# Block sums of the output weights by adding DMAs, a ring of seven weight blocks, and loads and stores issued by GpSimd, in a one-core attention and feed-forward kernel

## The chip, the cores and the metric

The kernel runs on one core of a Trainium2 chip. The metric is the device time of one execution in microseconds, the median of several runs. The core's engines are TensorE (PE, with its weight loads as PEld), VectorE (DVE), ScalarE (ACT), GpSimd (POOL) and SyncE (SP). Each works through its own list of instructions in order, and they wait for one another by semaphores. SP does no arithmetic here: it issues DMA transfers, which sixteen DMA engines carry out.

## The reference

```python
def _attn_ref(q, k, v, n_sink, window):          # q, k, v: (4, 8, 768, 64), n_sink 4, window 128
    scores = (1.0 / np.sqrt(D)) * np.matmul(q, k.transpose(0, 1, 3, 2))
    keep = is_sink | in_window                   # key < n_sink, or 0 <= query - key < window
    a = softmax(np.where(keep, scores, -1e9))    # with 1e-9 added to the sum
    return np.matmul(a, v)

def _moe_ref(x, w_in, w_out):                    # x: (3072, 512), w_in (512, 2048), w_out (2048, 512)
    h = x @ w_in
    return (h - np.tanh(h)) @ w_out
```

The weights come in as 64-bit words that the chip decodes to 32-bit floats. All products are made at nearly full float precision: an operand is split into a rounded high part and a low rest, and three of the four partial products are added.

## The kernel before

**Tiling.** The 3072 tokens are 12 chunks of 256 (`cc`), the hidden width is 8 groups of 256 (`g`). A step is one chunk with one group, and there are 96 steps in the order of the list `order`: chunks 0 to 2 interleaved in steps 0 to 23 while the weights are still being decoded, then chunks 3 to 11 one after the other with eight steps each. A step's first half is 24 matmuls into `h` (`mm1`, line 772). Then come tanh on ACT (791), the difference on DVE (794), the rounded high part on ACT (797 or 810) and the low part on DVE (800 or 813), and the second half multiplies by the group's block of `w_out`: 12 matmuls of 512 columns (`mm2`, 842) for chunks 0 to 4, 21 matmuls of 256 columns (`mm7`, 876) for chunks 5 to 11.

**Seven products.** `mm7` uses Strassen's scheme: seven block products in place of eight. It needs sums of the four quarter blocks of each group's `w_out` (`derive`). Five new blocks a group are made: three go into `edge` tiles, which take the place of decoded `w_in` groups that are no longer needed, and two replace quarters of `w` itself. Each sum is made on DVE or GpSimd with three adds over high and low parts (980, 982, 984) in half of the tile `wide`, rounded by ACT (996), and its low rest is made by DVE (1001, 1003).

**Weights.** `weights(k, g)` decodes `w_in` (k = 0) or `w_out` (k = 1) of a group: three DVE passes (156, 158, 160) into `wm`, one of two scratch halves of the tile `pt`, then the high part on ACT (712) and the low part on DVE (716). The decoded `w_in` is stored to DRAM (`wscr`, 720), and from step 24 on it is streamed back in four blocks of 256 KB a step into a ring of five block places (`stream`, 757): four in a tile `ring`, one in `spare`. A block feeds six `h` matmuls, and its place is free when these are done.

**Attention.** Each chunk has four units (pairs of heads). A unit loads keys and queries (`load_qk`, 333 and 342), from unit 12 on splits them (`split`: ACT 468 and 478, DVE 473 for keys, GpSimd 481 for the queries' low part), makes scores (509), softmax (524 to 560), the sink columns on GpSimd (569 to 571), transposes (594) and masks (608 on DVE, 614 on GpSimd); a chunk's values follow (657), and `x` for the chunk's steps.

**Order.** All of it is put down as work items with an engine, an estimated time and a due time (`work.add`). The class `Work` walks through them once, when the program is built, takes at each moment the item with the earliest due time on each engine, and so fixes one order for every engine. Times such as `STREAM`, `DEAR`, `LEAD` and `PACE` are due times; they move instructions in that order and have no other effect. SP issues every transfer, in this one order: weights, keys, queries, values, ring blocks, and stores of results. A transfer that waits for its place holds back all those behind it.

Of the kernel before, what the change touches and what calls it, by code (L numbers as in the profile page):

```python
# [32 lines left out]
NG = 8  # L33
# [135 lines left out]
class Work:  # L169
# [7 lines left out]
    def __init__(self, slack, pad, late):  # L177
        self.all, self.wrote, self.read = [], {}, {}
        self.slack, self.pad, self.late = slack, pad, late
# [14 lines left out]
    def order(self):  # L194
# [15 lines left out]
        while any(waiting.values()):  # L210
# [6 lines left out]
            if lands:  # L217
                free[e], done[n] = t + lands, t + lands + 1700
# [14 lines left out]
def _banded(tc, qd, kp, vp, vs, masks, w_in, w_out, ident, pts, early, out):  # L233
    nc = tc.nc
    et = mybir.EngineType
    with ExitStack() as ctx:
# [5 lines left out]
        qpool, kpool, vpool, hpool = pool("qpool", 2), pool("kpool", 2), pool("vpool", 3), pool("hpool", 1)  # L242
# [14 lines left out]
        spare = gpool.tile([P, WG // 2], F32R, tag="spare", name="spare")  # L257
        wscr = dpool.tile([NG, P, 2 * WG], F32, tag="wscr", name="wscr")
        kscr = dpool.tile([2, P, 2, DM // 2], F32, tag="kscr", name="kscr")
# [4 lines left out]
        work = Work(SLK, PAD, LATE)  # L264
# [8 lines left out]
        FIRST, EARLY, PACE, LEAD = 45000.0, 4600.0, 7956.0, 43418.0  # L273
        UNIT, SECOND, WLEAD, WNEXT = 2000.0, 3000.0, 6000.0, 2500.0
        HALF2, LAST = 9148.0, 6188.0
        SPILL, STREAM, DEAR, DLATE = 47526.0, 10850.0, 120000.0, 17426.0
# [20 lines left out]
        def raw(u):  # L297
            return u < RAW
# [16 lines left out]
        def slots(u):  # L315
            i = u if u < 2 or u in lent else u % 2 + 2
            return [("kt", i), ("qt", i)]

        def load_qk(u):
            cc, p, b, c = unit(u)  # L320

            def lend():
                if lent[u] not in place_of:
# [4 lines left out]
            def keys():  # L328
                if u in lent:
# [3 lines left out]
                nc.sync.dma_start(kt[u], kp[b, p, :, 2 * c * TS : 2 * c * TS + KW])  # L333

            def queries():
# [5 lines left out]
                else:  # L341
                    nc.sync.dma_start(qt[u], src.rearrange("h d s -> d h s"))

            def zeros():
                if u in lent:
# [8 lines left out]
            work.add("SP", 500, t, keys, (), [slots(u)[0], "seq k"], lands=800)  # L354
            work.add("SP", 1000, t, queries, (), [slots(u)[1], "seq q"], lands=600 if raw(u) else 1000)
# [3 lines left out]
        def load_v(cc):  # L359
# [19 lines left out]
            work.add("SP", 500 * took, due_unit(4 * cc), values, (), [vslot[cc, i] for i in new] + ["seq v"],  # L379
# [312 lines left out]
        def weights(k, g):  # L692
# [28 lines left out]

            d = due_group(g) + WNEXT * k - WLEAD
# [630 lines left out]
```

## Time and profile before

| | us |
|---|---|
| median of 3 runs (lowest, highest) | 696.69 (695.9, 698.17) |
| profiled execution | 696.93 |
| its span, first to last instruction | 695.2 |
| PE busy in it | 663.2 |
| DVE busy | 565.3 |
| ACT busy | 411.5 |
| GpSimd busy | 175.9 |

The profiled execution's own time is its span and 1.7 us around it. PE's share says that matmuls stand nearly back to back; where PE is not busy, the list of waits names the engine or transfer that let it go on ("issue" means that the trace names none). The tables by stretch show where along the span that is.

### The profile page before, as it was taken

To read this page: it belongs to the slowest core of one execution; us is meant where nothing else is said; L and a number is where in the kernel's file an instruction comes from. 1 tells how busy PE (TensorE), PEld (TensorE's weight loads), DVE (VectorE), ACT (ScalarE), POOL (GpSimd) and SP (SyncE) were. 2 spreads that over 40 slices of the span, in tenths; PEclk is the share of its full clock that TensorE was granted. 3 is DMA by queue.
4 is the path that set the end of the run, shared out by engine and by line. 5 is a ranking of instruction groups with operands and counts; after the bars stand their busy time and mean duration, and the time that the engine had idled before them with its cause. 6 is when DMAs were issued, how large, how long until landed. Compare 5 with 4: busy or idle time off the path is not lost.

```text
span 695.2 us, 14415 instructions
## 1 busy us (share of the span) xinstructions
PE 663.2 (95%) x5099; PEld 609.7 (88%) x5099; DVE 565.3 (81%) x1385; ACT 411.5 (59%) x1056; POOL 175.9 (25%) x287
## 2 busy tenths in 40 slices
PE   6899999999998997999999999999999999999996
PEld 4677899999987886889999999999999998999895
DVE  6999998946888999899988878978777986985554
ACT  5985333347885665766668567567566665662221
POOL 5433000002445563313223223221112132220000
PEclk9999999999999999999999999999999999999999
DMA  5779864241257575657757857856865865654762
GB/s 180 263 258 385 314 263 154 93 148 58 79 145 229 163 212 152 197 179 219 248 178 214 279 165 205 269 180 188 264 199 169 261 212 172 188 177 132 240 192 71
DMA packets 77485, 137.23 MB, mean 197 GB/s; under 512 B 8156, under 2 KB 28764, under 8 KB 77404
## 3 DMA queue, kind: packets, MB, share of 16 engines
q1 hardware_dynamic: 77404, 136.22, 62.8%
q8 instruction: 42, 0.69, 0.4%
q14 instruction: 39, 0.32, 0.1%
HBM read 120.98 MB, written 15.20 MB: 196 GB/s over the span
## 4 chain that ended last, share of the span: by engine, by line
PE 71%; DVE 14%; ACT 6%; DMA 5%; issue 2%; POOL 1%; SPq 0%; DVEq 0%; POOLq 0%; ACTq 0%
PE h L772 29%; PE s L876 10%; PE o L876 7%; PE o L842 6%; PE s L842 3%; PE x L657 3%; DMA ring<-wscr 3%; PE t L594 2%; PE t L657 2%; PE t L842 2%; PE x L842 2%; PE t L509 1%; PE x L509 1%; DVE wide L982 1%; PE s L509 1%
## 5 line engine op out<-in xcount | busy, mean ns | idle before, releaser
L772 PE MATMUL h<-xh,ring 128*128 128x256 f32 x924 | 185.4, 282 | 8.2 <-DMA ring<-wscr 5.0
L772 PEld LDWEIGHTS h<-xh,ring 128*128 128x128 f32 x924 | 150.9, 189 | 10.4 <-DMA ring<-wscr 6.3
L772 PE MATMUL h<-xl,ring 128*128 128x256 f32 x462 | 128.8, 279 | 0.0
L791 ACT ACTIVATE gbuf<-h 128x512 f32<-128x512 f32 x96 | 57.2, 596 | 104.9 <-PE h L772 59.0
L481 POOL TENSOR_TENSOR q<-qraw,q 128x512 fp32r<-128x512 f32 x36 | 47.6, 1321 | 247.3 <-ACT q L478 247.3
L772 PEld LDWEIGHTS h<-xl,ring 128*128 128x128 f32 x462 | 87.4, 189 | 0.3
L534 ACT ACTIVATE p<-p,st 128x132 f32<-128x132 f32 x168 | 67.0, 401 | 21.5 <-DVE st L526 19.8
L810 ACT CAST ghbuf<-gbuf 128x896 fp32r<-128x896 f32 x55 | 51.8, 943 | 41.4 <-DVE gbuf L807 41.2
L813 DVE TENSOR_TENSOR glbuf<-gbuf,ghbuf 128x896 fp32r<-128x896 f32 x55 | 62.0, 1128 | 14.7 <-ACT ghbuf L810 10.7
L772 PE MATMUL h<-xh,w 128*128 128x256 f32 x384 | 73.4, 281 | 0.0
L772 PEld LDWEIGHTS h<-xh,w 128*128 128x128 f32 x384 | 60.8, 188 | 1.3 <-PE x L657 0.2
L560 ACT ACTIVATE p<-p,st 128x132 f32<-128x132 f32 x168 | 54.2, 394 | 4.1 <-DVE st L555 3.5
L794 DVE TENSOR_TENSOR gbuf<-h,gbuf 128x512 f32<-128x512 f32 x55 | 37.9, 689 | 19.4 <-ACT gbuf L791 18.9
L772 PE MATMUL h<-xl,w 128*128 128x256 f32 x192 | 53.5, 279 | 0.0
L842 PE MATMUL o<-w,ghbuf 128*128 128x512 f32 x192 | 51.5, 399 | 1.3 <-ACT ghbuf L797 1.3
L473 DVE TENSOR_TENSOR ks<-kraw,ks 64x392 fp32r<-64x392 f32 x72 | 48.2, 670 | 5.0 <-ACT ks L468 2.7
L772 PE MATMUL h<-xh,spare 128*128 128x256 f32 x228 | 50.6, 285 | 1.3 <-DMA spare<-wscr 1.3
L614 POOL TENSOR_TENSOR pt<-pt,after 128x512 f32<-128x512 f32 x32 | 43.7, 1366 | 27.7 <-ACT pt L611 25.7
L608 DVE TENSOR_TENSOR pt<-t,below 128x512 f32<-128x512 f32 (+1 forms) x48 | 28.9, 601 | 19.5 <-ACT pt L611 7.9
L569 POOL CAST z<-p 128x16 fp32r<-128x16 f32 x42 | 11.0, 261 | 119.1 <-ACT p L560 116.2
L772 PEld LDWEIGHTS h<-xh,spare 128*128 128x128 f32 x228 | 39.0, 189 | 1.8 <-DMA spare<-wscr 1.5
L842 PEld LDWEIGHTS o<-w,ghbuf 128*128 128x128 f32 x192 | 33.6, 188 | 7.2 <-ACT ghbuf L797 1.5
(173 smaller groups left out, 1659.6 us busy)
## 6 DMA issues: line engine op xcount, KB each, us to landing
ring<-wscr SPq DMA_DIRECT2D x231, 256.0 KB, 4.0
spare<-wscr SPq DMA_DIRECT2D x57, 256.0 KB, 4.0
qraw<-qd SPq DMA_DIRECT2D x36, 256.0 KB, 3.9
wraw<-w_in SPq DMA_DIRECT2D x16, 512.0 KB, 7.0
wraw<-w_out SPq DMA_DIRECT2D x16, 512.0 KB, 8.2
wscr<-w SPq DMA_DIRECT2D x16, 512.0 KB, 6.8
kraw<-kp SPq DMA_DIRECT2D x38, 196.0 KB, 3.8
v<-vp SPq DMA_DIRECT2D x27, 256.0 KB, 3.2
```

Of the source, the lines that this page charges most:

```text
L473: (nc.gpsimd if KP else nc.vector).tensor_tensor(k[o, h, :], t[r, :], k[r, h, :].bitcast(F32), op=ALU.subtract)
L481: (nc.gpsimd if QP else nc.vector).tensor_tensor(ql[u], qt[u], qh[u].bitcast(F32), op=ALU.subtract)
L534: nc.scalar.activation(e, e, AF.Exp, bias=st[u][:, j : j + 1], scale=-1.0, accum_out=st[u][:, 4 + j : 5 + j],)
L560: nc.scalar.activation(pr[u][:, j, :], pr[u][:, j, :], AF.Copy, scale=s[:, 8 + j : 9 + j])
L614: nc.gpsimd.tensor_tensor(w[:, :, 0, :], w[:, :, 0, :], after.unsqueeze(1).to_broadcast([P, 4, P]), op=ALU.mult)
L772: nc.tensor.matmul(hps[n][:, f, :], lhsT=w, rhs=x, start=r == 0, stop=r == 11)
L791: nc.scalar.activation(g0, h(), AF.Tanh)
L794: nc.vector.tensor_tensor(g0 if strassen(n) else h(), h(), g0, op=ALU.subtract)
L810: nc.scalar.copy(ghbuf[:, n % 2], gbuf[:, 1:, :])
L813: nc.vector.tensor_tensor(glbuf[:, :7, :], gbuf[:, 1:, :], ghbuf[:, n % 2].bitcast(F32), op=ALU.subtract)
L842: nc.tensor.matmul(sums_of(n, cc, t), lhsT=a[:, f, t * P : (t + 1) * P], rhs=wt[1, g][:, (0, 1, 0)[i], f, :], start=first and not low and ...
L876: nc.tensor.matmul(acc, lhsT=a[:, b, :], rhs=factor(g, m, part % 2), start=g == 0 and part == 0 and m in (4, 1, 2, 7), stop=closes(n) and ...
```

## The change

Three things change, and the due times are set anew.

1. **Block sums by transfers.** While `w_out` of a group is being decoded, three transfers store the blocks that the sums need to a new DRAM scratch `bscr`: two straight from `wm` (`spill_plus`), and one after ACT has negated half of it into `gbuf` (`negative`, `spill_minus`). The next weight that is decoded into the same half of `pt` now waits for the first two of these to land. Later `derive` makes each sum with two transfers: SP copies one block from `bscr` into the sum's own place, GpSimd issues a second transfer that adds the other block to it. ACT rounds the result, DVE makes the low rest. The adds on DVE and GpSimd and their scratch in `wide` are gone.
2. **Ring of seven.** Three block places stand in the tile `spare`, four in `ring`. To make room, keys and queries have one buffer each in place of two, and unit u + 1 is loaded where u + 2 was.
3. **Other queues.** From unit 12 on keys and queries, from chunk 4 on values, the result stores of the seven-product part (all but the last chunk's) and the reload of the kept block (`keep(True)`) are issued by GpSimd. The queries' low part goes from GpSimd to DVE (`QP` 1 to 0).

```diff
-        qpool, kpool, vpool, hpool = pool("qpool", 2), pool("kpool", 2), pool("vpool", 3), pool("hpool", 1)
+        qpool, kpool, vpool, hpool = pool("qpool", 1), pool("kpool", 1), pool("vpool", 3), pool("hpool", 1)
...
-        SLK, PAD, LATE, QP, KP, BP, LEAD3 = 0.0, 1.05, 65222.0, 1, 0, 1, 37045.0
-        SA, NSLOT, RING, GP, DP = 5, 7, 5, 0, 1
+        SLK, PAD, LATE, LAND, QP, KP, BP, LEAD3 = 0.0, 1.05, 65222.0, 4372.0, 0, 0, 1, 89032.0
+        SA, NSLOT, RING, GP, LQ, ST = 5, 7, 7, 0, 1, 1
...
-                nc.sync.dma_start(kt[u], kp[b, p, :, 2 * c * TS : 2 * c * TS + KW])
+                (nc.gpsimd if LQ and not raw(u) else nc.sync).dma_start(kt[u], kp[b, p, :, 2 * c * TS : 2 * c * TS + KW])
...
-                    nc.sync.dma_start(qt[u], src.rearrange("h d s -> d h s"))
+                    (nc.gpsimd if LQ else nc.sync).dma_start(qt[u], src.rearrange("h d s -> d h s"))
...
-                    nc.sync.dma_start(vt[cc, i], vp[b, i * P : (i + 1) * P, :])
+                    (nc.gpsimd if LQ and cc > 3 else nc.sync).dma_start(vt[cc, i], vp[b, i * P : (i + 1) * P, :])
...
+            def negative():
+                nc.scalar.activation(gbuf[:, 4:].rearrange("p b t -> p (b t)"), wm[key][:, DM:], AF.Copy, scale=-1.0)
+
+            def spill_plus():
+                nc.sync.dma_start(bscr[g][:, 0:2], wm[key][:, :DM].rearrange("p (k c) -> p k c", k=2))
+                nc.sync.dma_start(bscr[g][:, 2], wm[key][:, 3 * DM // 2 :])
+
+            def spill_minus():
+                nc.sync.dma_start(bscr[g][:, 3:5], gbuf[:, 4:].rearrange("p (k a) t -> p k (a t)", k=2))
...
+            if k:
+                work.add("ACT", 520, d + 1600, negative, [("dw", r)], ["minus"])
+                work.add("SP", 700, d + 1500, spill_plus, [("dw", r)], [("b", g, 0)], lands=1200)
+                work.add("SP", 400, d + 2200, spill_minus, ["minus"], [("b", g, 1)], lands=800)
...
-            ring[i] = spare if i == 4 else ring["a"][:, i, :]
+            if i > 3 and "b" not in ring:
+                ring["b"] = gpool.tile([P, 3, WG // 2], F32R, tag="spare", name="spare")
+            ring[i] = ring["b"][:, i - 4, :] if i > 3 else ring["a"][:, i, :]
...
+            def copied():
+                nc.sync.dma_start(block(1).bitcast(F32), bscr[g][:, x])
+
+            def added():
+                nc.gpsimd.dma_start(block(1).bitcast(F32), bscr[g][:, y], accum_op=ALU.add)
+
+            def rounded():
+                nc.scalar.activation(block(0), block(1).bitcast(F32), AF.Copy, scale=-1.0 if m == 4 else 1.0)
+
+            def rest_of():
+                lo, hi = block(1), block(0).bitcast(F32)
+                if m == 4:
+                    nc.vector.scalar_tensor_tensor(lo, lo.bitcast(F32), -1.0, hi, op0=ALU.mult, op1=ALU.subtract)
                 else:
...
+                    nc.vector.tensor_tensor(lo, lo.bitcast(F32), hi, op=ALU.subtract)
...
-                if RAW <= u + 2 < NU:
-                    load_qk(u + 2)
+                if RAW <= u + 1 < NU:
+                    load_qk(u + 1)
```

SP's order while chunk 9 is worked on (steps 78 to 82 are being loaded; `spare` and `ring` are ring blocks, `qraw`, `kraw`, `v` and `out` the loads and stores of attention and results). Before:

```order
L757 DMA ring<-wscr 128x512 x4
L342 DMA qraw_6897<-qd 128x2x256
L333 DMA kraw_6918<-kp 128x392
L757 DMA spare<-wscr 128x512
L757 DMA ring<-wscr 128x512 x3
L376 DMA v_4_7007<-vp 128x512
L376 DMA v_5_7009<-vp 128x512
L757 DMA ring<-wscr 128x512
L757 DMA spare<-wscr 128x512
L342 DMA qraw_7105<-qd 128x2x256
L757 DMA ring<-wscr 128x512 x4
```

After, at the same place:

```order
L778 DMA ring<-wscr 128x512 x4
L778 DMA spare<-wscr 128x512 x3
L778 DMA ring<-wscr 128x512 x4
L778 DMA spare<-wscr 128x512 x3
L778 DMA ring<-wscr 128x512 x4
```

Every load that stood between ring blocks has gone to GpSimd's list, and SP holds ring blocks alone there.

DVE's order around step 29, chunk 3 (`s` scores, `h` and `glbuf` the step's difference and low part, `wide` the scratch of the block sums). Before:

```order
L800 TENSOR_TENSOR glbuf<-h_2624,ghbuf 128x512
L980 TENSOR_TENSOR wide<-w_3_1227 128x512
L982 TENSOR_TENSOR wide<-wide,w_3_1227 128x512
L984 TENSOR_TENSOR wide<-wide,w_3_1227 128x512
L1003 SCALAR_TENSOR_TENSOR edge_2660<-wide,edge_2660 128x256
L1001 TENSOR_TENSOR edge_2660<-wide,edge_2660 128x256 x2
L980 TENSOR_TENSOR wide<-w_4_1333 128x512
L673 TENSOR_TENSOR xl_2786<-x,xh_2785 128x512
```

After, at the same step:

```order
L815 TENSOR_TENSOR h_2775<-h_2775,gbuf 128x512
L613 TENSOR_TENSOR pt<-t,below 128x4x128
L559 TENSOR_SCALAR st_2854<-st_2854 128x4
L560 RECIPROCAL st_2854<-st_2854 128x4
L821 TENSOR_TENSOR glbuf<-h_2775,ghbuf 128x512
L486 TENSOR_TENSOR q_2887<-qraw_2814,q_2887 128x512
L478 TENSOR_TENSOR ks_2921<-kraw_2828,ks_2921 64x392 x2
```

The adds into `wide` are gone, the low rests of the edge blocks (24 of 256 columns) now stand at steps 20 to 28, and the queries' low part (486) has joined each unit.

GpSimd's order around steps 22 and 23, where the sums' transfers are issued (`edge` with 995 is an adding transfer, `z` the sink columns, 614 and 619 the mask multiplication before and after). Before:

```order
L481 TENSOR_TENSOR q_2115<-qraw_1958,q_2115 128x512
L569 CAST z<-p_2084 128x2x8
L570 TENSOR_TENSOR z<-p_2084,z 128x2x8
L571 CAST z<-z 128x2x16
L614 TENSOR_TENSOR pt<-pt,after 128x4x128
L481 TENSOR_TENSOR q_2211<-qraw_2050,q_2211 128x512
```

After:

```order
L337 DMA kraw_2139<-kp 128x392
L995 DMA edge_2072<-bscr 128x256
L574 CAST z<-p_2052 128x2x8
L575 TENSOR_TENSOR z<-p_2052,z 128x2x8
L576 CAST z<-z 128x2x16
L619 TENSOR_TENSOR pt<-pt,after 128x4x128
L995 DMA edge_2072<-bscr 128x256 x2
L346 DMA qraw_2225<-qd 128x2x256
L995 DMA edge_2072<-bscr 128x256
L995 DMA edge_2172<-bscr 128x256
L337 DMA kraw_2263<-kp 128x392
```

Transfers that wait for a landing or for PE now stand in one line with the sink columns and masks, on which the chunk's values wait.

## Rows read from the trace of the kernel before

**Rows 1.** The page of the profile: busy time of the engines with their share of the span.

```profile
PE 663.2 (95%) x5099; PEld 609.7 (88%) x5099; DVE 565.3 (81%) x1385; ACT 411.5 (59%) x1056; POOL 175.9 (25%) x287
```

**Rows 2.** Busy time by stretch: from and to (us from the span's start), length, then busy us and instructions of PE, PEld, DVE, ACT, POOL, the granted TensorE clock, the DMA engines' busy share and GB/s.

```profile
50.00:100.00 50.00, 48.91 (x333) 42.86 (x333) 46.90 (x72) 23.76 (x47) 6.69 (x10) 1.00 0.91 343
...
150.00:200.00 50.00, 49.93 (x352) 44.34 (x351) 34.47 (x106) 37.17 (x105) 14.76 (x24) 1.00 0.26 80
...
200.00:275.00 75.00, 68.20 (x466) 59.26 (x465) 69.39 (x155) 46.87 (x130) 41.91 (x53) 0.99 0.64 191
275.00:345.00 70.00, 69.14 (x500) 63.03 (x500) 62.28 (x156) 46.35 (x122) 18.75 (x25) 0.99 0.68 206
...
475.00:660.00 185.00, 177.75 (x1530) 171.86 (x1529) 142.81 (x358) 104.10 (x249) 33.35 (x54) 1.00 0.67 202
```

**Rows 3.** PE's waits between 200 and 345 us: who was waited for, us in total, times, longest.

```profile
PE h L772 <- issue: 3.1, 1, 3.1
PE s L509 <- DVE ks L473: 1.7, 3, 0.9
PE o L842 <- ACT ghbuf L797: 1.3, 1, 1.3
PE t L509 <- DVE pt L608: 0.9, 1, 0.9
```

**Rows 4.** The timeline between 258 and 276 us (start, us, instruction; in brackets the engine's idle time before it): block-sum adds on GpSimd and DVE, the step's low part, and PE's next matmuls into `h`.

```profile
268.49 1.10 POOL L980 TENSOR_TENSOR wide<-w 128x256 f32<-128x256 f32 x1 [2.83 <-DVE edge L1001]
...
270.05 1.11 DVE L980 TENSOR_TENSOR wide<-w 128x512 f32<-128x512 f32 x1
...
272.32 0.69 DVE L984 TENSOR_TENSOR wide<-wide,w 128x512 f32<-128x512 f32 x1
272.93 0.68 DVE L800 TENSOR_TENSOR glbuf<-h,ghbuf 128x512 fp32r<-128x512 f32 x1
...
273.72 0.55 PE L772 MATMUL h<-xh,ring 128*128 128x256 f32 x1 [3.13 <-issue]
```

**Rows 5.** The stretches around that wait (columns as in rows 2), and two pieces of the chain of work that ended last: start, us, what.

```profile
270.60:273.70 3.10, 0.00 (x0) 0.01 (x1) 3.03 (x5) 0.65 (x2) 1.06 (x2) 0.93 0.52 163
273.70:276.70 3.00, 2.98 (x14) 3.00 (x15) 2.54 (x10) 2.53 (x9) 0.00 (x0) 0.50 0.05 13
...
273.72 2.90 PE h L772 x12
...
277.20 1.41 PE h L772 x12
```

**Rows 6.** DVE's groups of instructions between 200 and 345 us: the block sums' adds and the edge blocks' low rests (count, busy us, mean ns, idle before).

```profile
L982 DVE TENSOR_TENSOR wide<-wide,w 128x512 f32<-128x512 f32 x16 | 14.8, 928 | 0.4
L984 DVE TENSOR_TENSOR wide<-wide,w 128x512 f32<-128x512 f32 x16 | 14.6, 911 | 0.5
...
L980 DVE TENSOR_TENSOR wide<-w 128x512 f32<-128x512 f32 x16 | 13.2, 826 | 1.1 <-DMA out<-wide 0.9
...
L1001 DVE TENSOR_TENSOR edge<-wide,edge 128x256 fp32r<-128x256 f32 x16 | 6.1, 418 | 0.0
```

**Rows 7.** PE's waits between 345 and 660 us.

```profile
PE h L772 <- DMA ring<-wscr: 5.0, 6, 1.5
PE s L876 <- ACT ghbuf L810: 1.4, 3, 0.5
PE h L772 <- DMA spare<-wscr: 1.3, 1, 1.3
```

**Rows 8.** SP's timeline between 577 and 588 us, ahead of one of those waits (start, time to issue, transfer).

```profile
578.98 0.33 SPq L757 DMA_DIRECT2D spare<-wscr  x1
582.32 0.38 SPq L342 DMA_DIRECT2D qraw<-qd  x1
582.80 2.11 SPq L757 DMA_DIRECT2D ring<-wscr  x4
```

**Rows 9.** What SP's own queue waited for between 345 and 660 us: the loads of values (376), keys (333) and queries (342).

```profile
SPq L376 <- PE t L657: 18.7, 5, 4.3
...
SPq L333 <- DVE ks L473: 11.8, 10, 2.3
SPq L342 <- POOL q L481: 10.0, 5, 3.0
```

**Rows 10.** GpSimd's groups: the queries' low parts and the masks over the whole span.

```profile
L481 POOL TENSOR_TENSOR q<-qraw,q 128x512 fp32r<-128x512 f32 x36 | 47.6, 1321 | 247.3 <-ACT q L478 247.3
L614 POOL TENSOR_TENSOR pt<-pt,after 128x512 f32<-128x512 f32 x32 | 43.7, 1366 | 27.7 <-ACT pt L611 25.7 <-DMA spare<-wscr 0.8 <-DMA ring<-wscr 0.7
```

**Rows 11.** Landing times: stores of decoded `w_in` issued between 60 and 100 us (count, KB, median us), and all transfers from and to `wscr` over the span.

```profile
wscr<-w SPq DMA_DIRECT2D x8, 512.0 KB, 9.4
...
DMA to landing us min/median/max: 2.6/4.0/10.7
```

**Rows 12.** DVE's timeline between 66 and 100 us: the ends of a `w_out` decode (160) and the first pass of the next one (156), groups 1 to 3.

```profile
66.80 1.28 DVE L160 SCALAR_TENSOR_TENSOR pt<-wraw,pt 128x1024 uint32<-128x1024 uint32 x1
...
75.34 0.68 DVE L156 TENSOR_SCALAR pt<-wraw 128x1024 uint32<-128x1024 uint32 x1
...
78.34 1.22 DVE L160 SCALAR_TENSOR_TENSOR pt<-wraw,pt 128x1024 uint32<-128x1024 uint32 x1
...
87.14 0.68 DVE L156 TENSOR_SCALAR pt<-wraw 128x1024 uint32<-128x1024 uint32 x1
```

More of the change, by code (lines that the diff above doesn't have):

```diff
@@ L217, in order @@
             if lands:
-                free[e], done[n] = t + lands, t + lands + 1700
+                free[e], done[n] = t + (took if e == "POOL" else lands), t + lands + (1700 if self.all[n][2] < self.late else self.land)
             if locks:
@@ L322, in lend @@
             def lend():
+                if u == 3:
+                    if u not in place_of:
+                        place_of[u] = gpool.tile([P, 3 * WG // 2], F32, tag="spare", name="qk3")
+                    return place_of[u]
                 if lent[u] not in place_of:
@@ L353, in load_qk @@
                 work.add("POOL", 460, t - ZL, zeros, (), [slots(u)[1]])
-            work.add("SP", 500, t, keys, (), [slots(u)[0], "seq k"], lands=800)
-            work.add("SP", 1000, t, queries, (), [slots(u)[1], "seq q"], lands=600 if raw(u) else 1000)
+            e = "POOL" if LQ and not raw(u) else "SP"
+            work.add(e, 600, t, keys, (), [slots(u)[0], "seq k"], lands=800 if raw(u) else 1000)
+            work.add(e, 800, t, queries, (), [slots(u)[1], "seq q"], lands=600 if raw(u) else 1000)
         vslot, vnew = {}, []
@@ L375, in values @@
                     vt[cc, i] = vpool.tile([P, DM], F32, tag="v", name=f"v{cc}_{i}")
-                    nc.sync.dma_start(vt[cc, i], vp[b, i * P : (i + 1) * P, :])
+                    (nc.gpsimd if LQ and cc > 3 else nc.sync).dma_start(vt[cc, i], vp[b, i * P : (i + 1) * P, :])
             took = len(new)
-            work.add("SP", 500 * took, due_unit(4 * cc), values, (), [vslot[cc, i] for i in new] + ["seq v"],
+            work.add("POOL" if LQ and cc > 3 else "SP", 500 * took, due_unit(4 * cc), values, (), [vslot[cc, i] for i in new] + ["seq v"],
                      lands=1000 * took)
@@ L942, in gather @@
                 for t in range(2):
-                    work.add("SP", 500, d + 1000, lambda t=t: put(t), o, (), lands=1000)
+                    work.add("POOL" if ST else "SP", 500, d + 1000, lambda t=t: put(t), o, (), lands=1000)
                 return
@@ L1015, in derive @@
                 if e not in opened:
                     opened.add(e)
-                    old.append(("w", 0, EDGE[e] or NSLOT))
+                    old += [("w", 0, EDGE[e] or NSLOT), ("edge", e)]
                 else:
-                    old.append(("edge", e))
-            new = [("edge", edge_at(g, x)[0]) for x in ((0,), (1, 2), ())[what]]
-            for k in range(3):
-                took = (700 if poolish else 330) if n == 1 else (1330 if poolish else 600)
-                work.add("POOL" if poolish else "DVE", took, d, lambda k=k: added(k), [("w", 1, g)], o, port=True)
@@ L1024, in derive @@
-            work.add("ACT", 340 * n, d, rounded, o, w + old)
-            work.add("DVE", 340 * n, d, rest_of, o, w, port=True)
+                    src.append(("edge", e))
+            took = 300 * n
+            work.add("SP", 400, d, copied, src, w + old, lands=took + 100)
+            work.add("POOL", 650, d, added, src, w, lands=1000 + 600 * n)
+            work.add("ACT", 360 * n, d, rounded, (), w)
+            work.add("DVE", 360 * n, d, rest_of, (), w, port=True)
         opened = set()
```

95 lines of the change are left out of this document (31 added, 64 removed).

## The prediction, made before the changed kernel ran

> **What bounds the kernel now.** I read the page's busy shares first, then the table by stretch, then PE's list of waits in two stretches, and from each wait went back to what stood in its way. PE is busy 663.2 us and is the bound [rows 1]; the change leaves its matmuls as they are, 5099 of the same shapes, so it can only give back PE's waits or add to them. Between 150 and 200 us PE is busy 49.93 of 50 us [rows 2]: nothing can be gained there, only lost. The waits in reach lie in two places.
>
> *Block sums, 200 to 345 us.* DVE is busy 69.39 of 75 us and 62.28 of 70 us there [rows 2], and PE waits 3.1 + 1.7 + 1.3 + 0.9 = 7.0 us [rows 3]. The wait of 3.1 us has no releaser in the list, so I went to the timeline. The matmuls into `h` that end it start at 273.72, right behind the DVE instruction that reads the bank they need (272.93 and 0.68 us long), and this one stood behind block-sum adds [rows 4]. DVE was busy 3.03 of these 3.10 us [rows 5]. After the wait, PE's granted clock was 0.50, the lower of its two levels (1.2 of 2.4 GHz), for three microseconds: twelve matmuls took 2.90 us, and 1.41 us a little later [rows 5]. So this stretch holds 7.0 + 1.5 = 8.5 us.
>
> *Ring blocks, 345 to 660 us.* PE waits 5.0 + 1.3 us for seven ring blocks [rows 7]. On SP's timeline one sees why: between 578.98 and 582.32 us SP issued nothing, then a load of queries, then the block that PE was waiting for [rows 8]. SP had been held by the load, which waits for its buffer: queries for GpSimd, keys for DVE, values for PE [rows 9]. Blocks whose place was free stood behind it.
>
> **The change part by part.** The sum starts from the profiled execution, 696.93 us, whose span is 695.2 us; the median of the runs shown is 696.69 us, so 0.2 us lie between the two and no correction is made.
>
> *Adds gone.* 48 adds leave DVE, 14.8 + 14.6 + 13.2 = 42.6 us of the 131.7 us that it was busy between 200 and 345 us [rows 2, 6]. The low rests stay (24 of about 0.42 us [rows 6], now at steps 20 to 28, and eight of 512 columns); about ten units' query parts come in at 0.69 us each, the price of a 512-column instruction without GpSimd beside it [rows 4] (beside GpSimd's adds the same shape took 1.11 us [rows 4]). Net some 30 us go from DVE, which then is near 100 of 145 us busy. The four DVE-made waits have no queue left to stand in. I take 8.0 us of the 8.5; the bounds are 8.5 and 3 (the single longest wait alone).
>
> *Loads off SP's list, ring of seven.* Each load that I found in front of a late block is one that the change moves. The two extra places add to that: a block may be fetched two blocks earlier, twelve matmuls or 1.41 us at least [rows 5], and the longest of these waits was 1.5 us [rows 7]. New in SP's list are eight copies for the sums of `w`, which wait for PE to finish with the block; they stand ahead of ring blocks around steps 33 to 40 and take back some of that lead. I take 5.5 of 6.3 us; bounds 6.3 and 0.
>
> A page of the Trainium skill speaks against this term. "DMA: Bandwidth & Descriptors", section "Issuing engines are not separate DMA queues", says that issuing from several engines saves only the sequencer's time to issue, since all transfers run on the same sixteen engines. The trace shows the time to issue, 0.38 us for the load of queries, and beside it 3 us in which SP stood [rows 8]. By that page of the Trainium skill the seven waits would give back at most 7 x 0.38 = 2.7 us, and the sum would end near 691; by the row it is the standing that goes. I take the row.
>
> *Stores while weights are decoded.* Three stores a group, 640 KB, join a stretch in which the DMA engines are already 91% busy and DVE is busy 46.90 of 50 us [rows 2]. The next weight in the same half of `pt` now waits for them. Before, a `w_out` decode ended at 68.08 and 79.56 us, and the next one began at 75.34 and 87.14 us: gaps of 7.3 and 7.6 us [rows 12]. A store issued there landed after 9.4 us [rows 11], so DVE would stand about 2 us twice, 4 us or so with a third group; once the weights are in, a landing takes 4.0 us [rows 11] and nothing is late. Behind the waiting pass stand the step's difference and low part, for which PE waits. But SP, held by these stores, also pushes fewer loads ahead, so the backlog that makes 9.4 us should be shorter. Price 2.0 us, bounds 0 and 6.
>
> *Query parts on DVE, late.* From 345 us on 20 units add 0.69 us each, 14 us in 315 us. Between 475 and 660 us DVE is busy 142.81 of 185 us [rows 2], so this is 77% going to some 82%. It stands in front of the chain of sums for which PE already waited three times, 1.4 us [rows 7]. Against that, GpSimd's 1.32 us per unit [rows 10] no longer slows DVE's instructions. Price 1.0 us, bounds -1 and 4.
>
> *GpSimd's list.* It loses 47.6 us of query parts [rows 10] and its share of the adds, and gains about 136 transfers. What GpSimd needs to issue one, no row shows. The nearest rows are SP's 0.38 us [rows 8] and GpSimd's own 1.32 us for an instruction of 512 columns [rows 10]; between them lie 52 and 180 us, on an engine that was busy 175.9 of 695 us [rows 1]. So its time is not the question, its order is: an adding transfer waits for the copy to land, and masks stand behind it. Price 1.5 us, bounds 0 and 16 (third rival). The accumulation itself is hidden: edge sums are issued from step 18 on and first used in step 40.
>
> ACT has 8 instructions more and 8 fewer; the head up to 50 us and the last 30 us keep their work. I cost these at nothing: PE is covered there by the same matmuls, or waits for what doesn't change.
>
> Sum: -8.0 - 5.5 + 2.0 + 1.0 + 1.5 = -9.0, so 696.9 - 9.0 = 687.9, say 688 us.
>
> **The rivals.** *Ring waits are the transfers' own.* If blocks are late because transfers run slowly, at a DMA share of 0.67 with bursts [rows 2], and not because SP stood, then only the time to issue comes back: 7 x 0.38 = 2.7 us in place of 5.5. That gives 691. For it speaks that the moved loads still share the DMA engines; against it, that SP visibly issued nothing for 3 us [rows 8]. This is also what that page of the Trainium skill would make of it.
>
> *DVE is only moved.* The stores hold DVE for the full 6 us in the decode stretch, and the query parts cost PE 4 us late. Then -8.0 - 5.5 + 6 + 4 + 1.5 = -2, or 695: no difference. For it: DVE had 3 us of slack in 50 there [rows 2]. Against it: decode runs ahead of PE, and the backlog should shrink.
>
> *GpSimd's order holds PE, and the kernel is slower.* Around steps 18 to 28, 24 adding transfers stand among the masks and sink columns of eight units. Each may go only when PE has freed the block and the copy has landed (2.6 to 4.0 us [rows 11]). Masks start before the change right when ACT is done with their input (25.7 of 27.7 us idle before them [rows 10]), so they have no lead over PE in this stretch, where PE waits for nothing [rows 2]. If each of eight masks waits half a landing, 2 us, PE loses 16 us, and the kernel ends at 688 + 16 - 1.5 = 702 us. It decides against the forecast as soon as the masks lose more than 9 us together. Against it: the order was made with a landing time of that size, and attention stands some four steps earlier after chunk 4.
>
> **How the numbers follow.** Forecast 688 (681 to 693): 0.56. Ring waits of their own, 691: 0.15. DVE only moved, 695: 0.13. GpSimd's order, 702: 0.16. A measurement of this kernel can tell about 0.3%, 2.1 us, from no change, so "same" is 694.6 to 698.8. Faster: 0.56 and 0.15 less a little at the edge, 0.70. Same: most of the third case, 0.11. Slower: the fourth and the rest, 0.19. The low end takes both gains in full and no cost but the late one at -1: 696.9 - 8.5 - 6.3 - 1 = 681. The high end, 700, covers the third case and the lower part of the fourth; some 0.13 lie above it and 0.05 below the low end.
>
> **What would show it.** Right: no `ring` or `spare` wait in PE's list after 345 us, SP's list waiting there for PE alone; DVE near 100 us busy between 200 and 345 us, and no stretch at granted clock 0.50 near 270 us; GpSimd busy or issuing well below its span. Wrong: a DVE wait at the decode's first pass for a `bscr` store (decode term), PE's waits for masks, values or transposes between 150 and 260 us (GpSimd's order), more waits for `ghbuf` after 345 us (query parts), or ring waits that stay although SP has issued the block early. The first thing that could upset the sum is GpSimd's time to issue, which no row here shows.

## The result, and the profile after

| | us |
|---|---|
| after, median of 4 runs (lowest, highest) | 685.78 (684.54, 688.15) |
| before, same chip, median of 4 runs | 696.68 |
| ratio, 95% interval | 0.9845 [0.9814, 0.9876] |
| profiled execution after, its span | 685.92, 684.2 |

The forecast was 688 in a range of 681 to 700; 10.9 us were gained where the sum had 9.0. Against the 0.3% that a measurement can tell, that is faster. (In the experiments below, one of the five executions of `queues_back` took 812.02 us at a mean granted clock of 0.752 and is left out of its median and ratio.)

The page of the kernel after, busy time of the engines (before: [rows 1]):

```profile
PE 665.0 (97%) x5099; PEld 613.8 (90%) x5099; DVE 531.4 (78%) x1365; ACT 412.7 (60%) x1056; POOL 204.7 (30%) x363
```

By stretch, columns as in [rows 2]:

```profile
50.00:100.00 50.00, 48.79 (x327) 42.39 (x326) 45.86 (x72) 25.59 (x53) 7.37 (x11) 1.00 0.84 276
...
150.00:200.00 50.00, 48.86 (x334) 43.00 (x334) 38.34 (x116) 39.10 (x113) 33.23 (x48) 1.00 0.81 192
200.00:275.00 75.00, 74.69 (x548) 66.29 (x546) 57.63 (x169) 57.12 (x161) 33.13 (x59) 1.00 0.77 230
275.00:345.00 70.00, 69.96 (x522) 63.85 (x519) 47.48 (x127) 43.86 (x112) 27.67 (x41) 1.00 0.90 260
...
475.00:660.00 185.00, 184.79 (x1590) 180.44 (x1589) 139.06 (x341) 97.06 (x218) 36.96 (x66) 1.00 0.68 209
```

In the middle DVE fell from 131.67 to 105.11 us and PE is idle 0.35 of 145 us where it was 7.66; late it is idle 0.21 of 185 us where it was 7.25. Between 150 and 200 us PE has lost: 1.14 us idle, 0.07 before. The span is 11.0 us shorter although PE's busy time grew, from 663.2 to 665.0 us with the same matmuls. That growth is the part which the prediction did not see.

PE's waits after, between 150 and 345 us (before: [rows 3]; `ghbuf` and `glbuf` are the high and the low part of a step's difference, `z` the sink columns, `ks` the split keys):

```profile
PE t L863 <- ACT ghbuf L818: 0.7, 1, 0.7
PE x L640 <- POOL z L576: 0.3, 1, 0.3
PE t L599 <- ACT p L565: 0.3, 1, 0.3
```

Between 345 and 660 us the list is empty (before: [rows 7]). What SP's queue waited for there, the two longest (before: [rows 9]):

```profile
SPq L778 <- PE h L793: 207.8, 164, 6.9
SPq L778 <- PE t L514: 19.5, 14, 9.5
```

SP waits for PE alone, as the prediction asked. DVE's waits between 50 and 110 us hold no first pass of a decode (156):

```profile
DVE h L815 <- ACT gbuf L812: 3.1, 6, 1.4
DVE pt L613 <- ACT pt L606: 0.8, 3, 0.3
DVE vsink L451 <- POOL vraw L447: 0.3, 1, 0.3
```

The stores for the sums land far sooner than the 9.4 us that I had assumed [rows 11]; the landing times after, by source and queue (count, KB, median us):

```profile
edge<-bscr SPq DMA_DIRECT2D x24, 128.0 KB, 4.0
edge<-bscr POOLq DMA_DIRECT2D x24, 128.0 KB, 4.7
...
bscr<-pt SPq DMA_DIRECT2D x8, 256.0 KB, 2.8
bscr<-gbuf SPq DMA_DIRECT2D x8, 256.0 KB, 2.0
w<-bscr SPq DMA_DIRECT2D x8, 256.0 KB, 4.3
w<-bscr POOLq DMA_DIRECT2D x8, 256.0 KB, 7.3
...
bscr<-pt SPq DMA_DIRECT2D x8, 128.0 KB, 3.2
```

GpSimd's groups after (count, busy us, mean ns, idle before): the issue time that no row of before showed.

```profile
L346 POOL DMA_DIRECT2D qraw<-qd x36 | 29.6, 821 | 222.7 <-DVE q L486 198.4 <-DVE st L560 9.3 <-ACT p L565 8.3
L995 POOL DMA_DIRECT2D edge<-bscr x24 | 24.1, 1279 | 9.7 <-PE s L863 9.6
...
L381 POOL DMA_DIRECT2D v<-vp x18 | 9.9, 557 | 19.7 <-PE t L662 19.2 <-issue 0.5
L995 POOL DMA_DIRECT2D w<-bscr x8 | 9.8, 1230 | 1.0 <-PE o L863 0.8
```

A plain load costs GpSimd 0.6 to 0.8 us, an adding transfer 1.0 to 1.2 us of its time (busy time by count; the mean of one is larger where two overlap).

### The profile page after: what moved, and what is told of

It reads as the page before. It is cut to its first block, busy times and chain, and to the rows that moved or that the text cites. A ratio compares the mean times of both kernels' runs of the same rounds, so it can differ in the third digit from the quotient of the medians.

```text
span 684.2 us, 14570 instructions
## 1 busy us (share of the span) xinstructions
PE 665.0 (97%) x5099; PEld 613.8 (90%) x5099; DVE 531.4 (78%) x1365; ACT 412.7 (60%) x1056; POOL 204.7 (30%) x363
## 4 chain that ended last, share of the span: by engine, by line
PE 83%; POOL 4%; DVE 4%; ACT 4%; DMA 2%; issue 2%; SPq 0%; POOLq 0%; DVEq 0%; ACTq 0%
PE h L793 35%; PE s L897 11%; PE o L897 8%; PE o L863 8%; PE x L662 3%; PE s L863 3%; PE t L599 2%; PE t L662 2%; PE t L514 2%; PE t L863 2%; PE x L514 2%; PE x L863 2%; POOL edge L995 1%; PE s L514 1%; DMA v<-vp 1%
## 5 line engine op out<-in xcount | busy, mean ns | idle before, releaser
L793 PE MATMUL h<-xh,ring 128*128 128x256 f32 x660 | 133.5, 282 | 0.0
L793 PEld LDWEIGHTS h<-xh,ring 128*128 128x128 f32 x660 | 107.8, 188 | 0.4 <-PE t L662 0.2
L793 PE MATMUL h<-xh,spare 128*128 128x256 f32 x492 | 100.0, 283 | 0.0
L346 POOL DMA_DIRECT2D qraw<-qd x36 | 29.6, 821 | 222.7 <-DVE q L486 198.4
L793 PE MATMUL h<-xl,ring 128*128 128x256 f32 x330 | 92.2, 279 | 0.0
L793 PEld LDWEIGHTS h<-xh,spare 128*128 128x128 f32 x492 | 81.0, 190 | 0.3
L793 PE MATMUL h<-xl,spare 128*128 128x256 f32 x246 | 69.4, 282 | 0.0
L793 PEld LDWEIGHTS h<-xl,ring 128*128 128x128 f32 x330 | 62.1, 188 | 0.3
L793 PEld LDWEIGHTS h<-xl,spare 128*128 128x128 f32 x246 | 46.7, 190 | 0.3
L815 DVE TENSOR_TENSOR h<-h,gbuf 128x512 f32<-128x512 f32 x41 | 28.5, 695 | 19.1 <-ACT gbuf L812 19.0
```

Of the source, the lines that this page charges most:

```text
L793: nc.tensor.matmul(hps[n][:, f, :], lhsT=w, rhs=x, start=r == 0, stop=r == 11)
L815: nc.vector.tensor_tensor(g0 if strassen(n) else h(), h(), g0, op=ALU.subtract)
```

## Experiments

All times are medians, all ratios are to the kernel before on the same chip.

| run | us | ratio, 95% interval |
|---|---|---|
| queues_back | 686.42 | 0.9864 [0.9834, 0.9893] |
| ring_five | 689.60 | 0.9895 [0.9872, 0.9918] |
| loads_on_gpsimd | 693.50 | 0.9966 [0.9948, 0.9984] |
| adds_left_out | 684.89 | 0.9839 [0.9810, 0.9868] |
| adds_back | 702.26 | 1.0081 [1.0058, 1.0104] |
| sums_alone | 703.88 | 1.0109 [1.0085, 1.0132] |
| old_due_times | 690.62 | 0.9908 [0.9884, 0.9933] |
| queues_and_ring_old_due | 704.99 | 1.0122 [1.0097, 1.0147] |
| adds_split | 704.36 | 1.0124 [1.0105, 1.0142] |
| before_shifted_96 | 700.67 | 1.0075 [1.0051, 1.0100] |
| before_shifted_64 | 701.26 | 1.0070 [1.0055, 1.0084] |
| shifted_back | 681.93 | 0.9794 [0.9779, 0.9809] |

### Ring or queues

**Queues back.** From the kernel after:

```diff
-        SA, NSLOT, RING, GP, LQ, ST = 5, 7, 7, 0, 1, 1
+        SA, NSLOT, RING, GP, LQ, ST = 5, 7, 7, 0, 0, 0
```

> The kernel after, with keys, queries, values, result stores and the kept block issued by SP again; the ring keeps seven places, the block sums keep their transfers. Theory 'SP stood' (the loads ahead of ring blocks made them late, the two extra places cover only a part): ring or spare waits come back in PE's list between 345 and 660 us, 2 to 6 us in all, SP's own queue waits there for DVE (ks) and PE (t) again, and the time is 688 to 692 us. Rival 'depth' (seven places are enough by themselves): SP waits for loads again, but PE shows at most 1 us of ring waits after 345 us, and the time stays at 685 to 687 us. The stretch 200 to 345 us should stay as after (PE waits under 1.5 us) by both.

PE has no wait at all between 345 and 660 us, and the interval of the ratio overlaps that of the kernel after. SP stood for loads as before:

```profile
SPq L346 <- DVE q L486: 12.4, 10, 2.7
SPq L337 <- DVE ks L478: 8.3, 11, 1.1
SPq L381 <- PE t L662: 7.3, 4, 3.3
```

So with seven places SP may stand for 28 us in all without a late block. "Depth" holds; beside seven places, moving the loads gave nothing that can be measured.

**Five places.** The same line with `RING` 5 and the loads on GpSimd.

> The kernel after, with five ring places in place of seven; loads and stores stay on GpSimd. Theory 'SP stood': with the loads gone from SP's list five places are enough, PE has at most 1 us of ring or spare waits between 345 and 660 us, and the time is 685 to 687 us. Rival 'depth': 4 to 6.3 us of these waits come back, 690 to 692 us. Rival 'the transfers are late themselves': the waits come back as well, and SP is seen to have issued the late block as soon as its place was free.

PE's waits between 345 and 660 us:

```profile
PE s L897 <- DVE glbuf L834: 2.0, 3, 0.7
PE h L793 <- DMA ring<-wscr: 0.4, 1, 0.4
```

0.9 us more for ring blocks lies before 345 us. Few ring waits, as "SP stood" has it, but the time is 3.8 us above the kernel after: neither expectation. The rest is in waits for the step's low part (2.0 us) and high part (0.6 us near 200 us), in an order that was made anew for five places. So five places are nearly enough for the ring itself (1.3 us of waits in all) where the later loads and the stores of results are off SP's list and the due times are the new ones.

**Loads on GpSimd alone**, in the kernel before:

```diff
-                nc.sync.dma_start(kt[u], kp[b, p, :, 2 * c * TS : 2 * c * TS + KW])
+                (nc.sync if raw(u) else nc.gpsimd).dma_start(kt[u], kp[b, p, :, 2 * c * TS : 2 * c * TS + KW])
...
-                    nc.sync.dma_start(qt[u], src.rearrange("h d s -> d h s"))
+                    nc.gpsimd.dma_start(qt[u], src.rearrange("h d s -> d h s"))
...
-                    nc.sync.dma_start(vt[cc, i], vp[b, i * P : (i + 1) * P, :])
+                    (nc.gpsimd if cc > 3 else nc.sync).dma_start(vt[cc, i], vp[b, i * P : (i + 1) * P, :])
```

> The kernel before with one edit: from unit 12 on keys and queries, from chunk 4 on values are issued by GpSimd instead of SP, each at its old place in the order; five ring places, adds on DVE and GpSimd. After the last runs I hold that either remedy is enough by itself: ring waits of 6.3 us fall to under 1.5 us between 345 and 660 us. Theory 'SP stood': they do, and the time falls by 3 to 6 us, to 690.5 to 693.5 us. Rival 'the loads stand in front of GpSimd's own work': the ring waits go, but PE waits as long for masks, sink columns or queries, 695 to 698 us. Rival 'the transfers are late themselves': ring waits stay above 4 us.

The ring waits fall from 6.3 to 3.4 us, not to 1.5, and 2.7 us are gained. The chain of work that ended last shows one of the five waits that are left (start, us, what):

```profile
577.29 0.69 PE h L772 x6
577.99 0.02 issue
578.00 4.00 DMA ring<-wscr
582.00 0.04 issue
582.05 0.97 PE h L772 x6
```

PE frees a place at 577.99, SP issues the block at 578.00, it lands 4.00 us later, and PE has used up the other four by then. With five places a block can be late though SP did nothing wrong. Three of the five waits, 2.0 us, are of this kind: the other two blocks were issued at 472.04 and 524.24, 0.02 us after their place was free, and landed 3.78 and 3.58 us later. The last two waits, 1.4 us at 647 and 650 us, follow the reload of the kept block and two stores of results, which this run leaves on SP. The first rival had 2.7 us for the loads term. By "DMA: Bandwidth & Descriptors", section "Issuing engines are not separate DMA queues", the Trainium skill gives issue time alone to moved loads; this run's gain agrees in size, though in the trace it is waits behind SP that went.

### Block sums

**Adds left out**, in the kernel before, with every engine's order as it was:

```diff
             def added(k):
+                return
```

> The kernel before, its order unchanged on every engine, with only the three adds of each block sum left out (so its products with block sums are of other numbers); ACT's rounding and DVE's low rests stay. Theory 'adds on DVE make the waits' (the prediction's first term): the waits of 7.0 us between 200 and 345 us and the stretch at low clock behind them go, the ring waits after 345 us stay, and the time falls by 7 to 9 us, to 687.5 to 690 us. Rival 'the waits move': without the adds the same waits come out later or at another engine, and less than 4 us is gained, 692.5 us or more.

By stretch (200 to 345 and 345 to 660 us):

```profile
200.00:345.00 145.00, 144.62 (x1059) 131.54 (x1059) 103.88 (x285) 100.35 (x273) 40.60 (x59) 1.00 0.69 214
345.00:660.00 315.00, 308.86 (x2695) 299.51 (x2692) 248.53 (x627) 186.74 (x447) 64.94 (x101) 1.00 0.67 206
```

PE's idle time in the first falls from 7.66 to 0.38 us, and its clock is 1.00; in the second it falls from 7.72 to 6.14 us. 11.3 us are gained: the first term's mechanism stands, and the adds cost somewhat more than the 8.5 us given to them.

**Adds back**, in the kernel after: the old `derive`, no stores while decoding, and the due times of the sums as before.

```diff
-        SPILL, STREAM, DEAR, DLATE = 54590.0, 4000.0, 39769.0, 31275.0
+        SPILL, STREAM, DEAR, DLATE = 54590.0, 4000.0, 120000.0, 17426.0
```

> The kernel after, with the block sums made by adds on DVE and GpSimd again (and their due times of before), without the stores of decoded blocks; queues and ring as after. Theory 'adds on DVE': DVE is busy 125 to 135 of 145 us between 200 and 345 us, PE waits there 5 to 9 us, one of them long with a stretch of low clock behind it, and the time is 691 to 695 us. Rival 'a place in the order': the waits of before were an accident of its order, with the new due times PE waits less than 3 us there, 686 to 688 us. The stretch 150 to 200 us should then lose its 1.7 us of waits, since GpSimd has no adding transfers there.

Slower than before. PE waits 13.6 us between 200 and 400 us, most of it as in [rows 3]:

```profile
PE h L793 <- issue: 6.6, 4, 2.7
PE o L863 <- ACT ghbuf L818: 3.5, 2, 2.6
```

The new due times start attention earlier, but that this makes the waits is not shown: with the old ones the same parts are no faster (`queues_and_ring_old_due`, 704.99 us). PE is busy 50.00 of 50 us between 150 and 200 us, so the 1.1 us that the kernel after loses there come with the new sums.

**Sums alone**, in the kernel before: `derive`, `negative` and the stores of the kernel after, with

```diff
-        SPILL, STREAM, DEAR, DLATE = 47526.0, 10850.0, 120000.0, 17426.0
+        SPILL, STREAM, DEAR, DLATE = 47526.0, 10850.0, 39769.0, 31275.0
```

> The kernel before, with the block sums made by transfers alone (stores while decoding, copy, adding transfer); five ring places, all other loads and stores on SP, the queries' low part on GpSimd. Theory 'two separate gains': the waits between 200 and 345 us fall from 7.0 us to under 2, the ring waits after 345 us stay at 5 to 8 us, and the time is 688 to 690 us. Rival 'GpSimd's order or SP's copies take it back': adding transfers among GpSimd's query parts and masks, or copies that wait for PE in front of ring blocks, cost 5 us or more, and the time is 694 us or above.

7.7 us slower than the kernel before. PE's waits between 345 and 660 us are now for ACT:

```profile
PE s L891 <- ACT ghbuf L825: 5.8, 8, 1.4
PE x L636 <- POOL z L572: 0.7, 1, 0.7
PE h L787 <- DMA ring<-wscr: 0.3, 1, 0.3
```

Between 200 and 225 us PE is busy 21.19 us at a mean granted clock of 0.86. The ring waits, which I expected to stay at 5 to 8 us with five places and all loads on SP, are 0.3 us, so they hang on the order too. Which instruction of the re-made order is to blame for the new waits was not tried.

**Due times.** The kernel after, and the kernel with adds back, with

```diff
-        SLK, PAD, LATE, LAND, QP, KP, BP, LEAD3 = 0.0, 1.05, 65222.0, 4372.0, 0, 0, 1, 89032.0
+        SLK, PAD, LATE, LAND, QP, KP, BP, LEAD3 = 0.0, 1.05, 65222.0, 4372.0, 0, 0, 1, 37045.0
...
-        FIRST, EARLY, PACE, LEAD = 45000.0, 4600.0, 8242.0, 72963.0
+        FIRST, EARLY, PACE, LEAD = 45000.0, 4600.0, 7956.0, 43418.0
...
-        HALF2, LAST = 8269.0, 4401.0
+        HALF2, LAST = 9148.0, 6188.0
```

and `SPILL`, `STREAM` as before.

> The kernel after with the due times of before (pace, lead of attention, second half, last step, stores of w_in, stream of ring blocks; those of the block sums as after). It tells how much of the gain is in the order that the new due times set. Theory 'the parts carry it': 685 to 689 us. Rival 'the order carries it': the block sums collide with attention as in the run of the sums alone (waits around 200 us, waits for ghbuf after 345 us), and the time is 695 us or above.

690.62 us, between both: 5.5 us below the kernel before with the parts alone, and 4.8 us above the kernel after.

> The kernel after with the block sums made by adds on DVE and GpSimd and all due times of before: so queues, ring of seven and the queries' part alone. Theory 'two separate gains': the waits of before between 200 and 345 us stay at about 7 us, the ring waits go, and the time is 689.5 to 692.5 us. Rival 'the order carries it': as slow as or slower than before, 696 us or above, with waits between 200 and 400 us of over 10 us as in the run with adds back (which had the new due times).

Queues and ring without the new sums lose 8.8 us to the kernel before, with 8.1 us of PE waits between 200 and 345 us. Some 3 to 4.5 us of it go to the layout and about 3 us to the clock, by the figures further down.

### GpSimd's list

**Adds split**, in the kernel after: each adding transfer in two (the sums of `w` by block; the edge blocks by halves, as shown):

```diff
-                nc.gpsimd.dma_start(block(1).bitcast(F32), bscr[g][:, y], accum_op=ALU.add)
+                for f in range(2):
+                    c = slice(f * HALF // 2, (f + 1) * HALF // 2)
+                    nc.gpsimd.dma_start(block(1)[:, c].bitcast(F32), bscr[g][:, y, c], accum_op=ALU.add)
```

> The kernel after with every adding transfer cut in two halves of the same total bytes, in the same place of the order: 64 in place of 32 on GpSimd. It doubles what GpSimd issues among the masks and sink columns; each issue took 1.23 to 1.28 us in the kernel after. Theory of the prediction's fourth rival in its small form ('GpSimd's list has little room between 180 and 260 us'): PE's waits for sink columns, masks and queries between 150 and 275 us grow by 2 to 8 us, and the time is 688 to 694 us. Rival 'GpSimd has room': they grow by less than 1 us, 685 to 687 us.

18.6 us slower than the kernel after, more than twice the worst that I expected. PE's waits between 150 and 275 us, and a table by stretch:

```profile
PE x L640 <- POOL z L576: 6.5, 1, 6.5
PE s L514 <- DVE ks L478: 4.7, 4, 2.7
```

```profile
185.00:200.00 15.00, 11.76 (x64) 10.52 (x63) 8.86 (x26) 9.66 (x30) 14.58 (x20) 0.77 0.82 156
200.00:215.00 15.00, 8.31 (x42) 6.41 (x42) 7.44 (x25) 7.62 (x22) 14.85 (x23) 0.77 0.64 116
```

GpSimd is busy 29.4 of 30 us: here it is the bound, sink columns and keys come late, and PE's granted clock falls to a mean of 0.77 besides. The kernel after has GpSimd at 45.03 of 60 us between 170 and 230 us.

### Where the buffers lie

PE's busy time rose with the same matmuls, so I took from the traces how far apart two matmuls of 256 columns start that follow each other directly (under 150 ns), as a mean over the trace. Before any buffer was shifted, every kernel made from the one after had 118.2 to 118.3 ns in the seven-product part, every one made from the one before 116.0 to 116.4, whatever its order or queues. What they share is the layout: with one key buffer fewer, all buffers behind it moved, and `x` and the step's parts (PE's stationary operand) begin at another byte of their partition. Decoded weights and ring begin 64 bytes beyond a multiple of 128 in all of them.

**Before, shifted by 96 and by 64 bytes:**

```diff
-                    vt[cc, i] = vpool.tile([P, DM], F32, tag="v", name=f"v{cc}_{i}")
+                    vt[cc, i] = vpool.tile([P, DM + 8], F32, tag="v", name=f"v{cc}_{i}")[:, :DM]
```

```diff
-                    kt[u] = kpool.tile([P, KW], F32, tag="kraw", name=f"kraw{u}")
+                    kt[u] = kpool.tile([P, KW + 4], F32, tag="kraw", name=f"kraw{u}")[:, :KW]
```

> The kernel before with eight floats more in each of the three value buffers and nothing else, so that x and the step's parts begin 96 bytes beyond a multiple of 128, as in the kernel after; order, queues and ring are as before. Theory 'the buffers' places': seven-product matmuls 118.3 ns instead of 116.4, ring 117.2 instead of 115.6, and the time rises by 4 to 6 us, to 700 to 702.5 us. Rival 'order or traffic': no matmul changes its pace, 695.5 to 697.5 us.

> The kernel before with four floats more in each of the two key buffers (laid out in units of 32 bytes, so 64 bytes in all) and nothing else: x and the step's parts begin 64 bytes beyond a multiple of 128, the same remainder that all decoded weights and the ring have; spare has it too. Theory 'same remainder is slowest': all groups go to about 119 ns, as spare before, and the time rises by 7 to 10 us, to 703.5 to 707 us. Rival 'only multiples of 64 matter': the pace stays at 116 ns, 695.5 to 697.5 us.

**Shifted back**, in the kernel after (the tile `spare` 16 floats longer to match):

```diff
-                    kt[u] = kpool.tile([P, KW], F32, tag="kraw", name=f"kraw{u}")
+                    kt[u] = kpool.tile([P, KW + 8], F32, tag="kraw", name=f"kraw{u}")[:, :KW]
...
-                ring["b"] = gpool.tile([P, 3, WG // 2], F32R, tag="spare", name="spare")
+                ring["b"] = gpool.tile([P, 3 * WG // 2 + 16], F32R, tag="spare", name="spare")[:, 16:].rearrange("p (i c) -> p i c", i=3)
```

> The kernel after with two pads in its tiles and nothing else: eight floats more in the key buffer, so that the buffers behind it (x, the step's high and low parts) begin at a multiple of 128 bytes in a partition again, as before the change, instead of 96 bytes beyond one; and sixteen floats ahead of the three spare ring places, so that these begin 64 bytes beyond a multiple of 128, as the other weights do. In all runs so far matmuls of 256 columns that stand back to back start 116.3 ns (seven-product part) and 115.6 ns (ring) apart with the buffers of before, 118.3 and 117.2 ns with those of after, whatever else was changed; from the spare place it is 119 ns with both. Theory 'the buffers' places set the pace of matmuls': seven-product part 116.4 ns, ring 115.7 ns, spare places under 117 ns, PE busy falls by 5 to 7 us, and the time is 678 to 681 us. Rival 'the pace belongs to the order or to the DMA traffic': it stays at 118, 117 and 119 ns, and the time at 685 to 687 us.

| kernel | x and parts, spare (bytes beyond a multiple of 128) | ring | spare | seven-product |
|---|---|---|---|---|
| before | 0, 0 | 115.6 | 119.0 | 116.4 |
| after | 96, 96 | 117.2 | 119.2 | 118.3 |
| before_shifted_96 | 96, 96 | 118.2 | 119.0 | 119.6 |
| before_shifted_64 | 64, 64 | 118.8 | 118.9 | 118.9 |
| shifted_back | 0, 64 | 116.5 | 115.8 | 116.2 |

(The last three columns are ns between two starts, by the moving operand.) The places do not fix the pace alone: `after` and `before_shifted_96` have the same remainders and differ by 1.0 and 1.3 ns in ring and seven-product part (counted beyond a multiple of 256, `x` and parts lie at 96 in the first and at 224 in the second), and the ring of `sums_alone`, laid out as before, has 116.5 ns where `before` has 115.6. The chain of work that ended last shows it directly, the 21 matmuls of one step's seven-product half from the first to the next `h`. After:

```profile
509.03 0.48 PE s L897 x4
...
511.52 0.24 PE h L793 x2
```

and shifted back:

```profile
508.15 0.47 PE s L897 x4
...
510.55 0.23 PE h L793 x2
```

2.49 against 2.40 us. The kernel before loses 4.5 and 5.1 us by a shift alone. Shifted by 96, with the same 5099 matmuls in the same order, PE's busy time is 671.8 us where it was 663.2 [rows 1]:

```profile
PE 671.8 (96%) x5099; PEld 619.4 (88%) x5099; DVE 566.1 (81%) x1385; ACT 411.9 (59%) x1056; POOL 176.4 (25%) x287
```

Shifted by 64 it is 672.6 us. Part of that comes back as shorter waits, PE's idle time between 345 and 660 us falling from 7.72 us to 4.86 and 4.99 us; so the time rises by less than PE's busy time, and by less than the 7 to 10 us expected of the second shift. The clock does not tell these kernels apart: their executions have a mean granted clock of 0.990 to 0.995, those of the kernel before on the same chip 0.990 to 0.995. The kernel after gains 3.9 us by the pads, and PE's busy time falls from 665.0 to 661.0 us:

```profile
PE 661.0 (97%) x5099; PEld 609.6 (89%) x5099; DVE 530.7 (78%) x1365; ACT 412.4 (61%) x1056; POOL 204.1 (30%) x363
```

That is 1 to 4 us short of what I expected (678 to 681); the ring came back only to 116.5 ns, and between 275 and 345 us PE waits 0.9 us for DVE ahead of scores, which it had not done. At 681.93 us this version beats both kernels.

## Why the prediction came out right, step by step

The accounting of the profiled executions, 11.0 us of span: PE's idle time fell by 7.3 us between 200 and 345 us and by 7.3 us from there to 660 us, the low clock behind the long wait went (1.5 us [rows 5]), and idle time grew by 1.1 us between 150 and 200 us, by 0.4 before 100 us and by 0.3 after 660 us. That makes 14.3, and 3.3 of it came back as slower matmuls.

- **Adds gone**, -8.0: measured 8.8 in place (7.3 idle, 1.5 clock), just above the upper bound of 8.5. The run with the adds left out, in the order of before, shows the mechanism; of its 11.3 us, 1.6 are shorter late waits, and 0.9 are not located.
- **Loads off SP's list, ring of seven**, -5.5: all 6.3 us of ring waits went, the upper bound. (The 7.3 us of idle time hold 1.4 us of waits for `ghbuf` besides, less 0.4 us of gaps that remain.) The size was near, the reason half wrong. I put it down to SP standing behind loads and gave the two places the second role. Moved loads alone gave 2.7 us, since in that order three of the five waits left are a block's own landing of 3.6 to 4.0 us; seven places with the loads left on SP do as well as both. The prediction's rows on SP were read rightly, but the row of [rows 8] shows one of seven waits, and I let it speak for all.
- **Stores while weights are decoded**, +2.0: nothing. DVE never waits for them. I had priced them by landings of the stretch before (9.4 us); they land in 2.0 to 3.2 us. PE's idle time between 50 and 100 us grew by 0.1 us.
- **Query parts on DVE, late**, +1.0: nothing after 345 us; the three waits for `ghbuf` [rows 7] went. The 0.7 us wait for `ghbuf` at 152 us stands behind a query part (0.69 us) and keys (1.15 us) on DVE, but the query part is not shown to make it: with the same instructions ahead and the old sums PE does not wait there (`adds_back`), and with the new sums and the query part on GpSimd it waits 1.2 us (`sums_alone`). It comes with the new sums; how was not traced.
- **GpSimd's list**, +1.5: of the 1.1 us lost between 150 and 200 us 0.3 us is a wait for sink columns behind its transfers. 136 issues took 106.6 us, between the bounds of 52 and 180. That "its time is not the question" does not hold: with 32 issues more, GpSimd's time is the bound.
- **What was not in the sum**: the buffers' places, +3.3 us by what is left over, 3.9 by the pads, 4.5 by shifting the kernel before (whose seven-product matmuls then go at 119.6 ns, those of the kernel after at 118.3). I took PE's matmuls as unchanged, "5099 of the same shapes"; their number was, their pace was not. This and 3.4 us of costs that did not come (1.1 of 4.5) nearly cancel, so the sum was right to 1.9 us partly by luck.

Of the rivals, "ring waits are the transfers' own" holds in part for the moved loads alone and falls with the ring of seven. "DVE is only moved" falls. "GpSimd's order" did not decide, but it was near: 32 issues more among the masks gave 704 us, where this rival had 702, though by GpSimd's busy time and not by masks that wait for a landing.

Why is each half slower than the kernel before? In the three runs PE is idle as long as before (32.0 us): 31.9 with adds back, 31.9 with queues and ring under the old due times, 31.5 with the sums alone. Each half removes waits, and others come. What grew is PE's busy time, by 6.0, 7.7 and 5.1 us. Part of it is the clock, here queues and ring under the old due times (columns and stretches as in [rows 2]):

```profile
200.00:275.00 75.00, 69.14 (x451) 59.93 (x450) 68.22 (x167) 48.98 (x138) 42.65 (x62) 0.95 0.59 183
275.00:345.00 70.00, 67.22 (x478) 61.09 (x477) 63.23 (x156) 45.64 (x124) 21.49 (x34) 0.98 0.67 205
```

PE was busy at the lower clock level for 3.0 us in the kernel before and for 6.2, 9.2 and 6.6 us in the three; half of the difference, 1.6, 3.1 and 1.8 us, is what that cost. The layout's 3.3 to 4.5 us make up the rest in the first two, as far as these figures go. The sums alone are laid out as before; some 3 us of theirs stay open, and so does why the waits moved. By the 4.8 us that the due times are worth with all parts in place, the order has a share in that, but no run separates it.

## What to carry to other kernels

Before crediting a moved queue, ask whether the late transfer could have come in time at all: the time from a free place to the landing against the work that the other places hold. Here two more places did alone what the queue was moved for. When a buffer is dropped or resized, see where the buffers behind it now begin, and whether PE's busy time for the same matmuls changed: two pads, of 8 and 16 floats, were worth 4 us here. And GpSimd's time to issue counts like work: in a stretch where GpSimd was three quarters busy PE waited 0.3 us behind its transfers; with GpSimd fully busy there the kernel took 19 us more.

## What the hardware showed beyond the expected

**Operand places.** Matmuls of 256 columns started 115.6 to 116.9 ns apart (means of the groups by moving operand: decoded `w_in`, ring, spare, seven-product part) where the stationary operand began at a multiple of 128 bytes and the moving one 64 bytes beyond, and 117.1 to 119.6 ns in every other combination that ran (0 with 0, 64 with 64, 96 with 64, 96 with 96). Whether the distance of the two or the place of one decides was not separated, and equal remainders gave up to 1.3 ns of difference; the pads also moved values, queries and scores. The Trainium skill, "TensorE: Matmul & The Clock Gate", section "Step-by-step: what each phase is for", says that PE reads the streaming operand and the weights through two independent ports, so that loading weights takes nothing from a running matmul. These runs show the pace to depend by 1 to 3% on where the two operands lie; whether the weight loads take that time from the matmuls, against the Trainium skill, no run shows.

**Adding transfers.** 128 KB landed 4.7 us after GpSimd issued them (a copy by SP 4.0), 256 KB after 7.3 us (copy 4.3); cut in halves of 64 KB they still took 4.6 us to land and 1.0 us of GpSimd each.
